# Two adjacent PSUM banks for a tile's attention values, one reciprocal and one product out of them

## The chip, the cores and the metric

The kernel runs on one core of one Trainium2 chip. A core has a matmul engine (TensorE, PE in the profile), three engines for the other arithmetic (VectorE is DVE, ScalarE is ACT, GpSimd is POOL) and SyncE (SP), which here issues transfers. The engines run side by side, each through its own list of instructions in order, and wait for each other through semaphores. TensorE writes its results into PSUM, which has eight banks of [128, 512] float32; VectorE and ScalarE carry them out to SBUF. The metric is the device time of one execution in microseconds.

## The reference

Attention with a window of 128 positions and 4 sink positions, for 4 batches, 8 heads, 768 positions and head size 64, then a normalised two-layer network with a residual:

```python
scores = scale * np.matmul(q, k.transpose(0, 1, 3, 2))
keep = is_sink | in_window            # position < 4, or 0 <= rel < 128
scores = np.where(keep, scores, -1000000000.0)
a = np.exp(scores - np.max(scores, axis=-1, keepdims=True))
a = a / (np.sum(a, axis=-1, keepdims=True) + 1e-09)
x = np.matmul(a, v)                   # then the 8 heads side by side: 512 columns
...
xn = (x - mu) / np.sqrt(var + 1e-06) * g_ln
return x + np.maximum(xn @ w_ch1, 0.0) @ w_ch2     # 512 -> 2048 -> 512
```

## The kernel before

The 3072 rows (4 batches of 768) are 24 tiles of 128 rows; two tiles are a chunk, so there are 12 chunks, three to a batch. Everything is written out, no loop is left in the program.

**Attention.** From tile 6 on, `block(t)` (L941) issues one step of TensorE for two tiles at once: the values of tile t - 1 and the scores of tile t. The scores go into two tiles of PSUM called `pair`, two banks each (L1008, L1016); ScalarE takes their exponential (L1026) and VectorE multiplies it with the band mask (L1031). The values (L981, L988, L997) go into two one-bank tiles of PSUM from the ring `one`, four heads in each: 4 x 65 columns, of which the 65th of each head is the sum of the weights. VectorE takes the reciprocal of these sums (L1049) and multiplies the values with it (L1051), for each half of the heads on its own. Then follow the statistics (L902, L904), the power on POOL (L913), the normalised row xc (L916) and, through a transposing transfer, the input `xnt` of the network. The step is named sc or sv with the tile's number, its readers rc and x. The first tiles take other functions (`attend_tile`, `attend` and `value`, L861); for tiles 4 and 5 `value` already puts both halves into one `pair` tile and empties it with one reciprocal and one product (L892, L894).

**The network.** `mlp(c)` (L1056) computes the first product of a chunk in eight groups ph of 8 matmuls (L1067), each group in one `one` bank, each emptied by a relu rl (L1078 on ScalarE, L1080 on VectorE) into `h`. The second product is done plainly for the first three chunks (L1214, emptied at L1223 with the residual in the same instruction), and for the chunks after them in seven products P1 to P7 of half the size (`second_by_seven`, L1087; matmuls at L1118). Their operands are sums of halves of `h` (s1 to s4, L1095) and of the weights (w2t, L1258, in the buffers natf and natp). Three `one` banks hold the products; copies k1, k6, k5 and o12 (L1125) and sums o11, o22, o21 (L1129) empty them, and o (L1159) adds the residual.

**Banks.** PSUM is wholly given out: banks 0 to 3 are two `pair` tiles, banks 4 to 7 four `one` tiles, each a tile of its own (L414). Value halves, groups ph, products P, transposes and other small things share the four `one` tiles.

**The order.** Nothing of the order is fixed by hand. Every step is registered with `P.op` with its engine or engines, a priority, what it reads and writes and the buffers it holds. `Plan.run` (L116) then walks through planned time with planned durations, takes the step that is ready (or the best by priority within a short window) on the engine that comes first, and gives it a slot of each ring that it needs. `Plan.lat` (L108) says how long after its producer a step may begin in the plan; `PAR` (L236) holds the priorities and allowances. The result is one order for each engine and the choice of ScalarE or VectorE for steps that either can do. The layer below writes the instructions in that order and gives each the semaphore waits that follow from what earlier instructions did with the same tile. The plan's own times are not in the program.

Of the kernel before, what the change touches and what calls it, by code (L numbers as in the profile page):

```python
# [7 lines left out]
FP32 = mybir.dt.float32  # L8
BF16 = mybir.dt.bfloat16
AF = mybir.ActivationFunctionType  # L10
ALU = mybir.AluOpType
# [54 lines left out]
class Plan:  # L66
# [41 lines left out]
    def lat(self, src, dst):  # L108
        if src.eng == "PE" and src.dma is None:
            return -self.PE_DRAIN if dst == "PE" else self.SEM  # L110
        late = PAR["late"].get(src.name[:3], 0.0) if src.dma is not None and dst == "PE" else 0.0
        return late + (self.TO_PE if dst == "PE" else self.SEM)

    WINDOW = {"PE": 0.3, "ACT": 0.25, "DVE": 0.25, "POOL": 0.25, "SP": 0.0}

# [92 lines left out]
def dve(n, per=1.04):  # L208
    t = 0.067 + 0.001 * per * n
    return (t, t + 0.09)  # L210


def fix(occ, extra=0.09):
    return (occ, occ + extra)
# [18 lines left out]
NEVER = -1e9  # L233
BIG = 3.3e38

PAR = dict(late={"trx": 2.5, "trk": 2.5, "trq": 2.5, "w2l": 0.5}, solo={8: 4.0, 10: 4.0}, bh=12, k_nb={(5, "k", 0): 53.0, (5, "k", 1): 53.0, (5, "q", 0): 53.0, (5, "q", 1): 53.0}, vs1=33.0, s4=0.9, w2t_pool=0, cut=(1, 2), rs_nb={4: 48.0, 5: 48.0}, v_nb={8: 49.0, 9: 52.0}, last7=1, opool=0, gk=(5, 4), gv=(4, 5), strict=400.0, win=0.4, tr=-8.0, sc=-5.0, sc1=-2.0, av=2.0, blk=-8.0, step=8.0, trx=9.0, by_dma=4, x_by_dma=3,  # L236
           w1p=(1.6, 2.6, 2.7, 2.8), pm=3, w2p=(4.5, 4.51, 4.52, 4.53), apart=2, vs0=(2.0, 13.0), by_tile=0, vp=(0.0, 0.1, 2.0, 2.1, 4.55, 4.56), ld1=0.05, t0=0.8, warm=7.9, pm0=-40.0, w1g=17.0, gtt=1.25, seven=3, lead=(0, 0, 0, 2, 6, 8), w2t=-4.0, at7=(0.5, 1.5, 2.5, 3.5, 4.5, 6.5, 7.5))


def general(tc, nc, slots, pairs, ones, ident_f, ident, w1, w2, mhalf, g_s, g_r, q, k, v, out, scale):  # L240
# [133 lines left out]
def kernel(  # L374
# [12 lines left out]
    nc = tc.nc  # L387
# [18 lines left out]
    psum = ctx.enter_context(tc.tile_pool(name="psum", bufs=1, space=bass.MemoryType.PSUM))  # L406
    P = Plan()

    def ring(name, n, shape, dtype, pool=consts):
        P.ring(name, [Slot(pool.tile(shape, dtype, name=f"{name}{i}"), f"{name}{i}") for i in range(n)])  # L410

    banks = [Unit() for _ in range(8)]
    pairs = [psum.tile([128, 2, 512], FP32, name=f"pair{i}") for i in range(2)]
    ones = [psum.tile([128, 512], FP32, name=f"one{i}") for i in range(4)]  # L414
    P.ring("pair", [Slot(pairs[i], f"pair{i}", banks[2 * i:2 * i + 2]) for i in range(2)])
    P.ring("one", [Slot(ones[i], f"one{i}", [banks[4 + i]]) for i in range(4)])
    ring("natf", 2, [128, H, 2, 64], FP32)
    ring("natc", 4, [128, 2, 4, 64], BF16)
    ring("nat", 8, [128, H, 64], BF16)
# [36 lines left out]
    rec, low = const("rec", [128, NT, H], FP32), const("low", [128, NT, H], FP32)  # L456
# [16 lines left out]
    V, G = nc.vector, nc.gpsimd  # L473
# [44 lines left out]
    def negs(e):  # L518
# [9 lines left out]
        op=ALU.add, axis=mybir.AxisListType.X), ["ident"], writes=[Bc["sel"]])  # L528
# [8 lines left out]
         writes=[gr_b], dma=HW_T)  # L537
    P.op("gtt", pe(0.1), PAR["gtt"], lambda e: nc.tensor.transpose(gt_p.t[:, 0:NDM], g_rows, ident_f[0:NDM, 0:NDM]),
         reads=[gr_b, Bc["ident_f"]], writes=[gt_p])
    P.op("gtc", {"DVE": fix(0.07)}, PAR["gtt"] + 0.1, lambda e: V.tensor_copy(gt, gt_p.t[:, 0:NDM]), reads=[gt_p], writes=[Bc["gt"]])  # L540
    for h in range(H):
# [3 lines left out]
            reads=[Bc["vc"]], writes=[Bc["vcd"]], nb=3.5 + 0.55 * h)  # L545
    for b in range(B):
# [4 lines left out]
            reads=[Bc["vcd"], Bc["vc"], Bc["sel4" if b else "sel"]], writes=[Bvs[b]], nb=PAR["vs0"][1] if b == 0 else PAR["vs1"] if b == 1 else 40.0 * b)  # L551
# [14 lines left out]
    for c in range(4):  # L566
        P.op(f"w2ld{c}", {"POOL": (0.75, 0.8)}, PAR["w2p"][c], lambda e, c=c: G.dma_start(
            w2[c], moe_w_ch2[512 * c:512 * (c + 1), :].rearrange("(t p) n -> p t n", p=128)),
            writes=[Bw2[c]], dma=SW_W)
# [371 lines left out]
    def block(t, what="both"):  # L941
# [20 lines left out]
            hold += pes + ([held["ps", c]] if sinks else [])  # L962
        if last:
            lc, li, lb, lr = (t - 1) // 2, (t - 1) % 2, (t - 1) // RB, (t - 1) % RB
            po = [Buf(f"po{t - 1}{u}", "one") for u in range(2)]
            reads += last["pes"] + ([last["ps"], Bvs[lb], Bvt[lb]] if last["ps"] else [])
            reads += [vn_b[u] for u in ([t - 2, t - 1, t] if lr else [t - 1, t])]
            writes[:0] = po
            po[1].lag = 0.1
            for j, pp in enumerate(pps if fresh else ()):  # L970
                pp.lag = (0.5 if last["ps"] else 0.4) + 0.15 * j
            hold += last["made"]
# [4 lines left out]
        def go(e):  # L977
            for h in [4 * u + i for i in range(4) for u in range(2)] if last else ():
                pe_, col = at_p(h // 4, h)
                rs = slice(0, 128) if lr else slice(64 * (h // 4), 64 * (h // 4) + 64)  # L980
                nc.tensor.matmul(po[h // 4].t[:, 65 * (h % 4):65 * (h % 4) + 65], lhsT=pe_[rs, col:col + 128],  # L981
                                 rhs=vn_b[t - 1].t[rs, h, :], start=h % 4 == 0, stop=True, skip_group_check=True)
            if last and last["ps"]:
                for u in range(2):
                    for qh in range(2):
                        g = qh ^ u
                        rs = slice(64 * g, 64 * g + 64)
                        nc.tensor.matmul(po[u].t[64 * qh:64 * qh + 64, 0:260],  # L988
                                         lhsT=last["ps"].t[rs, 128 * u + 64 * li:128 * u + 64 * li + 64],
                                         rhs=(vs if g == u else vs_s)[lb][rs].rearrange("p h c -> p (h c)"),  # L990
                                         start=False, stop=True, skip_group_check=True)
            for h in [4 * u + i for i in range(4) for u in range(2)] if last else ():
                for qh in (0, 1) if lr else (1,):
                    g = qh ^ (h // 4)
                    rs = slice(64 * g, 64 * g + 64)
                    pe_, col = at_p(h // 4, h)
                    nc.tensor.matmul(po[h // 4].t[64 * qh:64 * qh + 64, 65 * (h % 4):65 * (h % 4) + 65],  # L997
                                     lhsT=pe_[rs, col + 128:col + 192], rhs=vn_b[t if qh else t - 2].t[rs, h, :],
                                     start=False, stop=True, skip_group_check=True)
            if not fresh:  # L1000
                return
            for hp in range(HP):
                u, col = hp // 2, 192 * (hp % 2)
                for g, kt, k0, c0, q0, n in ((u, kT, own, 0, own, 128), *([(1 - u, kprev, old + 64, 0, own, 128)] if r else []),
                                             *([(u, kprev, old, 128, own, 64)] if r else []), (1 - u, kT, own + 64, 128, own + 64, 64)):
                    for h2 in range(2):
                        rs = slice(64 * h2, 64 * h2 + 64)
                        nc.tensor.matmul(pps[u].t[64 * g:64 * g + 64, h2, col + c0:col + c0 + n],  # L1008
                                         lhsT=kt.t[rs, hp, k0:k0 + 64], rhs=qT.t[rs, hp, q0:q0 + n],
                                         start=col == 0 and c0 == (128 if g != u and not r else 0), stop=True, skip_group_check=True)  # L1010
            if sinks:
                for hp in range(HP):
                    for qh in range(2):
                        u = hp // 2
                        p0 = 64 * (qh ^ u) + 32 * (hp % 2)
                        nc.tensor.matmul(pps[1].t[p0:p0 + 32, u, 384 + 64 * (not r):512], lhsT=kts_b[b].t[:, hp, :],  # L1016
                                         rhs=qT.t[:, hp, :].rearrange("p (i u c) -> p u i c", i=2, u=2)[:, qh, 0 if r else 1:2],
                                         start=True, stop=True, skip_group_check=True)
# [21 lines left out]
        if last:  # L1040
            st, x, xc = last["made"]
            x_b[t - 1], xst_b[t - 1] = x, st
            rcb = Buf(f"rcb{t - 1}")
            recs.append(rcb)
            for u in range(2):
                one_rc = Buf(f"rc{t - 1}{u}")
                pv = lambda u=u: po[u].t[:, 0:260].rearrange("p (h c) -> p h c", c=65)
                rc = lambda u=u: rec[:, t - 1, 4 * u:4 * u + 4]
                P.op(f"rc{t - 1}{u}", {"DVE": fix(0.115)}, d + 0.05 + 0.002 * u, lambda e, rc=rc, pv=pv: V.reciprocal(rc(), pv()[:, :, 64]),  # L1049
                     reads=[po[u]], writes=[rcb, one_rc])  # L1050
                P.op(f"x{t - 1}{u}", {"DVE": dve(256)}, d + 0.051 + 0.002 * u, lambda e, u=u, rc=rc, pv=pv: V.tensor_tensor(  # L1051
                    x.t[:, 256 * u:256 * u + 256].rearrange("p (h c) -> p h c", c=64), pv()[:, :, 0:64],
                    rc().unsqueeze(2).to_broadcast([128, 4, 64]), op=ALU.mult), reads=[po[u], one_rc], writes=[x])
            normalise(lc, li, d - 0.06, st, x, xc)

    def mlp(c):  # L1056
# [238 lines left out]
    t = PAR["t0"]  # L1295
# [67 lines left out]
```

## Time and profile before

| | |
|---|---|
| median of 3 runs | 212.18 us (211.47 to 212.77) |
| the profiled execution | 212.08 us, of which the span from first to last instruction is 210.5 us |
| TensorE, weight loads | 202.9 us busy (96%), 169.8 us (81%) |
| VectorE, ScalarE, POOL | 163.0, 116.7, 115.3 us busy |
| granted TensorE clock | 1.000 on average |
| chain that ended last | 80% TensorE, 11% VectorE |

In the rows shown below, a row of the chain has the start and the duration in microseconds, the engine, the tile that is written, the source line and the number of instructions. A row of the groups has line, engine, operation, output <- input with partitions x elements and type, the count, then busy time in us and the mean of one in ns, then the idle time in front of them and what ended it. A row of the timeline has start, duration, engine, line and operation, and in brackets the idle time before it and its releaser. Buffer numbers are left out of names: `one` stands for each of the four.

### The profile page before, as it was taken

How to read it: one execution, taken by the hardware profiler on the slowest of the kernel's cores; microseconds unless marked ns; L12 is line 12 of the kernel's file. 1: busy time of each engine (PE TensorE's matmuls, PEld its weight loads, DVE VectorE, ACT ScalarE, POOL GpSimd, SP SyncE). 2: the span in 40 equal slices, each digit the busy share in tenths (PEclk: the TensorE clock that was granted, in tenths of full speed). 3: DMA queues.
4: the chain of work that ended last, by engine and by line, in shares of the span. 5: the costliest groups of instructions: out<-in, count | busy, mean ns of one | idle time of the engine just before them, and what ended most of it. 6: DMA issues, size and time to landing. Idle time of an engine off the chain costs nothing.

```text
span 210.5 us, 7217 instructions
## 1 busy us (share of the span) xinstructions
PE 202.9 (96%) x2971; PEld 169.8 (81%) x2971; DVE 163.0 (77%) x440; ACT 116.7 (55%) x204; POOL 115.3 (55%) x170
## 2 busy tenths in 40 slices
PE   7899999999999999999999999999999999999992
PEld 2557885678888888888888888888888888888881
DVE  5599764899889768888788788988888888863472
ACT  3788786343897175464564564573563663453610
POOL 7879842479699984855766765675542022310000
PEclk9999999999999999999999999999999999999999
DMA  5999999999999999999999999999997310310202
GB/s 152 189 185 201 190 206 203 170 168 116 153 166 148 152 186 133 98 220 129 78 182 128 103 194 117 110 200 121 129 171 67 125 29 3 128 25 0 103 25 84
DMA packets 104557, 27.82 MB, mean 132 GB/s; under 512 B 93764, under 2 KB 101576, under 8 KB 104520
## 3 DMA queue, kind: packets, MB, share of 16 engines
q0 software_dynamic: 70960, 13.18, 96.2%
q1 hardware_dynamic: 32360, 13.35, 38.1%
q10 hardware_dynamic: 1200, 0.79, 1.3%
q8 instruction: 24, 0.39, 0.8%
q14 instruction: 13, 0.11, 0.2%
HBM read 27.43 MB, written 6.29 MB: 160 GB/s over the span
## 4 chain that ended last, share of the span: by engine, by line
PE 80%; DVE 11%; DMA 3%; POOL 2%; issue 1%; ACT 1%; ACTq 0%; DVEq 0%; POOLq 0%
PE one L1067 38%; PE one L1118 23%; PE one L1214 7%; PE pair L1008 3%; DMA natf<-in_q_dram 3%; DVE st L902 2%; PE one L981 2%; PE one L988 2%; DVE x L1051 1%; DVE x L894 1%; POOL st L913 1%; PE one L997 1%; DVE ot L1223 1%; PE one L879 1%; DVE xc L909 1%
## 5 line engine op out<-in xcount | busy, mean ns | idle before, releaser
L1067 PE MATMUL one<-xnt,w 128*128 128x256 bf16 x768 | 88.8, 273 | 0.7 <-DVE ot L1223 0.5
L1067 PEld LDWEIGHTS <-w 128*128 128x128 bf16 x768 | 73.9, 98 | 10.6 <-issue 0.9
L1078 ACT ACTIVATE h<-one 128x512 bf16<-128x512 f32 x86 | 51.3, 598 | 37.9 <-PE one L1067 33.4
L666 POOL DMA_DIRECT2D vn<-in_v_dram x59 | 39.3, 687 | 10.1 <-DMA w<-in_moe_w_ch_dram 7.5
L912 POOL TENSOR_SCALAR st<-st 128x1 f32<-128x1 f32 x24 | 9.0, 376 | 48.2 <-DVE st L904 47.6
L1026 ACT ACTIVATE pe<-pair 128x768 bf16<-128x768 f32 x36 | 27.2, 809 | 13.4 <-PE pair L1008 13.1
L1118 PEld LDWEIGHTS <-h 128*128 128x128 bf16 x216 | 20.5, 98 | 3.4 <-issue 0.5
L1214 PE MATMUL one<-w,h 128*128 128x256 bf16 (+1 forms) x160 | 23.1, 294 | 0.0
L1118 PEld LDWEIGHTS <-sb 128*128 128x128 bf16 x176 | 17.1, 98 | 2.1 <-DVE sb L1095 0.2
L1214 PEld LDWEIGHTS <-h 128*128 128x128 bf16 x160 | 15.1, 98 | 4.6
L1118 PE MATMUL one<-w,h 128*128 128x256 bf16 x144 | 18.7, 273 | 0.0
L1125 ACT COPY tx<-one 128x256 f32<-128x256 f32 x17 | 6.3, 372 | 22.4 <-PE one L1118 22.4
L913 POOL TENSOR_TENSOR st<-st,mhalf 128x1 f32<-128x1 f32 x24 | 16.5, 688 | 2.0
L902 DVE BATCH_NORM_STATS2 st<-x 128x6 f32<-128x512 bf16 x24 | 16.7, 694 | 0.8
L1051 DVE TENSOR_TENSOR x<-one,rec 128x256 bf16<-128x256 f32 x36 | 15.2, 421 | 0.9
L724 POOL DMA_DIRECT2D nat<-in_k_dram x16 | 15.0, 939 | 1.3 <-DMA natp<-in_q_dram 1.3
L724 POOL DMA_DIRECT2D nat<-in_q_dram x16 | 14.2, 899 | 0.0
L1159 DVE TENSOR_TENSOR ot<-ot,x 128x512 f32<-128x512 f32 x15 | 10.4, 692 | 4.3 <-ACT ot L1125 4.0
L916 DVE TENSOR_SCALAR xc<-x,st 128x512 bf16<-128x512 bf16 x18 | 7.4, 412 | 8.0 <-POOL st L913 7.9
L1031 DVE TENSOR_TENSOR pe<-pe,band 128x768 bf16<-128x768 bf16 x24 | 12.1, 541 | 1.3 <-ACT pe L1026 1.2
L1118 PE MATMUL one<-natf,sb 128*128 128x256 bf16 x92 | 12.5, 273 | 0.0
L1118 PEld LDWEIGHTS <-natc 128*128 128x128 bf16 x112 | 10.9, 98 | 1.4 <-DVE natc L1095 0.2
(149 smaller groups left out, 305.2 us busy)
## 6 DMA issues: line engine op xcount, KB each, us to landing
out_dram<-ot SPq DMA_DIRECT2D x22, 256.0 KB
w<-in_moe_w_ch_dram POOLq DMA_DIRECT2D x6, 512.0 KB, 12.6
nat<-in_k_dram POOLq DMA_DIRECT2D x16, 128.0 KB, 4.5
nat<-in_q_dram POOLq DMA_DIRECT2D x16, 128.0 KB, 6.7
vn<-in_v_dram POOLq DMA_DIRECT2D x44, 32.0 KB, 5.3
w<-in_moe_w_ch_dram POOLq DMA_DIRECT2D x4, 256.0 KB, 11.1
vn<-in_v_dram POOLq DMA_DIRECT2D x15, 64.0 KB, 5.2
natp<-in_k_dram POOLq DMA_DIRECT2D x3, 256.0 KB, 12.3
```

The lines of the kernel that those rows point to most:

```text
L666: P.op(f"vld{t}_{i}", {"POOL": (0.8, 0.85)}, prio + 0.001 * i, lambda e, p0=p0, n=n, hs=hs, src=src: G.dma_start(m.t[p0:p0 + n, hs, 0:64], ...
L724: lambda e, nat=nat, ap=ap: G.dma_start(nat.t, ap), writes=[nat], dma=SW_N, after=gate(c), nb=PAR["k_nb"].get((c, nm, i), 0.0))
L902: P.op(f"bn{t}", {"DVE": fix(0.60)}, d + 0.12, lambda e: V.bn_stats(st.t[:, 8:14], x.t), reads=[x], writes=[st, mv])
L913: G.tensor_tensor(st.t[:, 16:17], st.t[:, 17:18], mhalf, op=ALU.pow)),
L1026: nc.scalar.activation(pes[j].t.rearrange("p a b -> p (a b)")[:, 0:768].rearrange("p (a b) -> p a b", a=2), pps[j].t[:, :, 0:384], AF.Exp, ...
L1031: V.tensor_mul(at_s, at_s, band[j] if r > 1 else edge[r][j].unsqueeze(1).to_broadcast([128, 4, 192]))
L1051: P.op(f"x{t - 1}{u}", {"DVE": dve(256)}, d + 0.051 + 0.002 * u, lambda e, u=u, rc=rc, pv=pv: V.tensor_tensor(x.t[:, 256 * u:256 * u + 256 ...
L1067: nc.tensor.matmul(ph.t[:, 256 * s:256 * s + 256], lhsT=w1[ht // 4][:, j, 128 * (ht % 4):128 * (ht % 4 + 1)], rhs=xnt.t[:, j, :], start=j ...
L1078: nc.scalar.activation(dst, ph.t, AF.Relu)
L1118: nc.tensor.matmul(bank.t[:, 0:256], lhsT=left[p](m)[:, a, :], rhs=right[p](m)[:, a, :], start=new and m + a == 0, stop=m + a == 4, skip_g ...
L1159: V if e == "DVE" else G).tensor_tensor(ot[i].t, ot[i].t, x.t, op=ALU.add), reads=[ot[i], *oo[i], x], writes=[done])
L1214: nc.tensor.matmul(pc.t[:, part], lhsT=h1[s].t[:, 256 * ii + 128 * i:256 * ii + 128 * i + 128], rhs=w2[s][:, ii, sl.start + part.start:sl. ...
```

## The change

The four one-bank tiles become slices of one tile `four` of four banks, and a third ring `two` on the same banks has its three adjacent pairs. A tile's values (from tile 6 on) take one slot of `two` instead of two slots of `one`, and leave it by one reciprocal of [128, 8] and one product of [128, 512] instead of two of each. In the plan, a step of TensorE that reads what VectorE or ScalarE made is set 0.15 or 0.1 us later (after planned time 24); one that reads a transposing transfer is set 0.5 us earlier; the priority of a chunk's second block moves by 1 and that of the weight sums by 4.

```diff
+        slack = PAR["slack"].get(src.eng, 0.0) if src.dma is None and dst == "PE" and src.start > 24.0 else 0.0
-        return late + (self.TO_PE if dst == "PE" else self.SEM)
+        return late + slack + (self.TO_PE if dst == "PE" else self.SEM)
...
-PAR = dict(late={"trx": 2.5, "trk": 2.5, "trq": 2.5, "w2l": 0.5}, ... step=8.0, ... w2t=-4.0, ...)
+PAR = dict(slack={'DVE':.15,'ACT':.1}, late={"trx": 2.0, "trk": 2.0, "trq": 2.0, "w2l": 0.5}, ... step=9.0, ... w2t=-8.0, ...)
...
-    ones = [psum.tile([128, 512], FP32, name=f"one{i}") for i in range(4)]
+    four = psum.tile([128, 4, 512], FP32, name="four")
+    ones = [four[:, i, :] for i in range(4)]
     P.ring("pair", [Slot(pairs[i], f"pair{i}", banks[2 * i:2 * i + 2]) for i in range(2)])
     P.ring("one", [Slot(ones[i], f"one{i}", [banks[4 + i]]) for i in range(4)])
+    P.ring("two", [Slot(four[:, i:i + 2, :], f"two{i}", banks[4 + i:6 + i]) for i in range(3)])
...
-            po = [Buf(f"po{t - 1}{u}", "one") for u in range(2)]
+            po = Buf(f"po{t - 1}", "two")
...
-            writes[:0] = po
-            po[1].lag = 0.1
+            writes[:0] = [po]
...
-                nc.tensor.matmul(po[h // 4].t[:, 65 * (h % 4):65 * (h % 4) + 65], lhsT=pe_[rs, col:col + 128],
+                nc.tensor.matmul(po.t[:, h // 4, 65 * (h % 4):65 * (h % 4) + 65], lhsT=pe_[rs, col:col + 128],
...
-            for u in range(2):
-                one_rc = Buf(f"rc{t - 1}{u}")
-                pv = lambda u=u: po[u].t[:, 0:260].rearrange("p (h c) -> p h c", c=65)
-                rc = lambda u=u: rec[:, t - 1, 4 * u:4 * u + 4]
-                P.op(f"rc{t - 1}{u}", {"DVE": fix(0.115)}, d + 0.05 + 0.002 * u, lambda e, rc=rc, pv=pv: V.reciprocal(rc(), pv()[:, :, 64]),
-                     reads=[po[u]], writes=[rcb, one_rc])
-                P.op(f"x{t - 1}{u}", {"DVE": dve(256)}, d + 0.051 + 0.002 * u, lambda e, u=u, rc=rc, pv=pv: V.tensor_tensor(
-                    x.t[:, 256 * u:256 * u + 256].rearrange("p (h c) -> p h c", c=64), pv()[:, :, 0:64],
-                    rc().unsqueeze(2).to_broadcast([128, 4, 64]), op=ALU.mult), reads=[po[u], one_rc], writes=[x])
+            one_rc = Buf(f"rc{t - 1}")
+            pv = lambda: po.t[:, :, 0:260].rearrange("p a (h c) -> p a h c", c=65)
+            rc = lambda: rec[:, t - 1, :].rearrange("p (a h) -> p a h", a=2)
+            P.op(f"rc{t - 1}", {"DVE": fix(0.13)}, d + 0.05, lambda e: V.reciprocal(rc(), pv()[:, :, :, 64]), reads=[po], writes=[rcb, one_rc])
+            P.op(f"x{t - 1}", {"DVE": dve(512)}, d + 0.051, lambda e: V.tensor_tensor(
+                x.t.rearrange("p (a h c) -> p a h c", a=2, c=64), pv()[:, :, :, 0:64],
+                rc().unsqueeze(3).to_broadcast([128, 2, 4, 64]), op=ALU.mult), reads=[po, one_rc], writes=[x])
```

More of the change, by code (lines that the diff above doesn't have):

```diff
@@ L234 @@
 BIG = 3.3e38
-PAR = dict(late={"trx": 2.5, "trk": 2.5, "trq": 2.5, "w2l": 0.5}, solo={8: 4.0, 10: 4.0}, bh=12, k_nb={(5, "k", 0): 53.0, (5, "k", 1): 53.0, (5, "q", 0): 53.0, (5, "q", 1): 53.0}, vs1=33.0, s4=0.9, w2t_pool=0, cut=(1, 2), rs_nb={4: 48.0, 5: 48.0}, v_nb={8: 49.0, 9: 52.0}, last7=1, opool=0, gk=(5, 4), gv=(4, 5), strict=400.0, win=0.4, tr=-8.0, sc=-5.0, sc1=-2.0, av=2.0, blk=-8.0, step=8.0, trx=9.0, by_dma=4, x_by_dma=3,
-           w1p=(1.6, 2.6, 2.7, 2.8), pm=3, w2p=(4.5, 4.51, 4.52, 4.53), apart=2, vs0=(2.0, 13.0), by_tile=0, vp=(0.0, 0.1, 2.0, 2.1, 4.55, 4.56), ld1=0.05, t0=0.8, warm=7.9, pm0=-40.0, w1g=17.0, gtt=1.25, seven=3, lead=(0, 0, 0, 2, 6, 8), w2t=-4.0, at7=(0.5, 1.5, 2.5, 3.5, 4.5, 6.5, 7.5))
+PAR = dict(slack={'DVE':.15,'ACT':.1}, late={"trx": 2.0, "trk": 2.0, "trq": 2.0, "w2l": 0.5}, solo={8:4.0,10:4.0}, bh=12, k_nb={(5, "k", 0): 53.0, (5, "k", 1): 53.0, (5, "q", 0): 53.0, (5, "q", 1): 53.0}, vs1=33.0, s4=0.9, w2t_pool=0, cut=(1, 2), rs_nb={4: 48.0, 5: 48.0}, v_nb={8: 49.0, 9: 52.0}, last7=1, opool=0, gk=(5, 4), gv=(4, 5), strict=400.0, win=0.4, tr=-8.0, sc=-5.0, sc1=-2.0, av=2.0, blk=-8.0, step=9.0, trx=9.0, by_dma=4, x_by_dma=3,
+           w1p=(1.6, 2.6, 2.7, 2.8), pm=3, w2p=(4.5, 4.51, 4.52, 4.53), apart=2, vs0=(2.0, 13.0), by_tile=0, vp=(0.0, 0.1, 2.0, 2.1, 4.55, 4.56), ld1=0.05, t0=0.8, warm=7.9, pm0=-40.0, w1g=17.0, gtt=1.25, seven=3, lead=(0,0,0,2,6,8), w2t=-8.0, at7=(0.5, 1.5, 2.5, 3.5, 4.5, 6.5, 7.5))
 def general(tc, nc, slots, pairs, ones, ident_f, ident, w1, w2, mhalf, g_s, g_r, q, k, v, out, scale):
@@ L987, in go @@
                         rs = slice(64 * g, 64 * g + 64)
-                        nc.tensor.matmul(po[u].t[64 * qh:64 * qh + 64, 0:260],
+                        nc.tensor.matmul(po.t[64 * qh:64 * qh + 64, u, 0:260],
                                          lhsT=last["ps"].t[rs, 128 * u + 64 * li:128 * u + 64 * li + 64],
@@ L996, in go @@
                     pe_, col = at_p(h // 4, h)
-                    nc.tensor.matmul(po[h // 4].t[64 * qh:64 * qh + 64, 65 * (h % 4):65 * (h % 4) + 65],
+                    nc.tensor.matmul(po.t[64 * qh:64 * qh + 64, h // 4, 65 * (h % 4):65 * (h % 4) + 65],
                                      lhsT=pe_[rs, col + 128:col + 192], rhs=vn_b[t if qh else t - 2].t[rs, h, :],
```

## The prediction

> **What bounds the kernel now.** I read the page's table of engines first, then the chain of work that ended last, then the timeline of one chunk.
>
> ```profile
> span 210.5 us, 7217 instructions
> PE 202.9 (96%) x2971; PEld 169.8 (81%) x2971; DVE 163.0 (77%) x440; ACT 116.7 (55%) x204; POOL 115.3 (55%) x170
> ```
>
> ```profile
> 17.60 0.43 PE one L1067 x3
> ...
> 56.86 0.67 DVE ot L1223
> 57.57 3.65 PE one L1067 x32
> ...
> 88.51 6.22 PE one L1067 x56
> ...
> 104.09 6.22 PE one L1067 x56
> ...
> 119.02 0.35 PE pair L1008 x32
> 119.37 0.23 PE pair L1016 x8
> 119.59 6.22 PE one L1067 x56
> ...
> 134.87 6.22 PE one L1067 x56
> ...
> 150.46 6.22 PE one L1067 x56
> ...
> 165.96 6.22 PE one L1067 x56
> ...
> 180.88 6.22 PE one L1067 x56
> ...
> 206.35 0.43 DVE ot L1168
> ```
>
> The columns are start, duration, engine, tile and line. From 88.51 to 180.88 the chain is TensorE and little else: six chunks in 92.37 us, some 15.4 each. TensorE is the bound, and every other engine works beside it. What lets it run on is that four one-bank tiles rotate:
>
> ```profile
> 104.03 6.29 PE L1067 MATMUL one<-xnt,w 128*128 128x256 bf16 x56
> ...
> 105.11 0.69 DVE L1080 TENSOR_SCALAR h<-one 128x512 bf16<-128x512 f32 x1 [0.37 <-PE one L1067]
> ...
> 105.99 0.60 ACT L1078 ACTIVATE h<-one 128x512 bf16<-128x512 f32 x1 [0.41 <-PE one L1067]
> ```
>
> TensorE writes 56 matmuls, seven groups of 8, without a pause, one step each (6.29 - 0.27) / 55 = 0.109 us (0.27 is one matmul's own length, below). A group is 0.87 us. VectorE and ScalarE empty finished groups meanwhile, each in a bank that TensorE is not filling. The first reader starts at 105.11; group one ended by the model at 104.03 + 7 x 0.109 + 0.27 = 105.06. So a hand-off from TensorE costs 0.04 us behind the drain of a last matmul, which is 0.27 - 0.11 = 0.16. The way back is in the chain above: 56.86 + 0.67 = 57.53, and TensorE starts at 57.57, again 0.04. A full turn costs 0.16 + 0.04 + 0.04 = 0.24 us beside the reader.
>
> **The change part by part.** The merged reciprocal and product are the small part. Readers' prices, by the groups of instructions (busy, mean ns):
>
> ```profile
> L1067 PE MATMUL one<-xnt,w 128*128 128x256 bf16 x768 | 88.8, 273 | 0.7 <-DVE ot L1223 0.5 <-issue 0.2
> L1078 ACT ACTIVATE h<-one 128x512 bf16<-128x512 f32 x86 | 51.3, 598 | 37.9 <-PE one L1067 33.4 <-DVE sb L1095 1.3 <-DVE st L902 1.1
> L1051 DVE TENSOR_TENSOR x<-one,rec 128x256 bf16<-128x256 f32 x36 | 15.2, 421 | 0.9
> L1129 DVE TENSOR_TENSOR ot<-one,tx 128x256 f32<-128x256 f32 x24 | 9.4, 417 | 2.4 <-PE one L1118 1.6 <-ACT tx L1125 0.9
> L1080 DVE TENSOR_SCALAR h<-one 128x512 bf16<-128x512 f32 x10 | 6.9, 690 | 3.1 <-ACT qT L671 1.5 <-PE one L1067 1.5
> L1125 ACT COPY tx<-one 128x256 f32<-128x256 f32 x17 | 6.3, 372 | 22.4 <-PE one L1118 22.4
> L1049 DVE RECIPROCAL rec<-one 128x4 f32<-128x4 f32 x36 | 6.2, 173 | 0.5 <-PE one L997 0.4
> L1223 DVE SCALAR_TENSOR_TENSOR ot<-one,st,x 128x512 f32<-128x512 f32 x6 | 4.5, 744 | 0.6 <-PE one L1214 0.5
> L894 DVE TENSOR_TENSOR x<-pair,rec 128x512 bf16<-128x512 f32 x2 | 1.4, 691 | 0.1
> L892 DVE RECIPROCAL rec<-pair 128x8 f32<-128x8 f32 x2 | 0.4, 194 | 0.0
> ```
>
> Before, a tile costs 2 x (0.173 + 0.421) = 1.19 us of VectorE; the merged form is already there for two tiles, 0.194 + 0.691 = 0.89. Over 18 tiles that is 18 x 0.30 = 5.4 us of an engine that is not the bound. The plan's parameters move every odd block (scores of tile 13, say) behind P1, the last operand sum s4 in front of reciprocal and product, the weight sums (w2t) some steps forward, and seven copies k1 from VectorE to ScalarE; TensorE's 2971 matmuls stay the same. What this could win is TensorE's own stalls: 134.87 to 150.46 (15.59) has the work of 119.59 to 134.87 (15.28) and takes 0.31 longer, 88.51 to 104.09 (15.58) has one such place more, and the products at 57.57 begin 0.48 late. Together some 1.1 us. On the queues of SP and POOL six transfers and one pair of small POOL operations change places with a neighbour, each with chunks of lead: nothing.
>
> **The large part is the tile itself.** The four banks are now one tile of [128, 4, 512], of which the old names are slices. The waits that the built programs carry, resolved to the operation that gives the awaited count (P, ph: products; rl, k, o, x: readers; the bank in brackets):
>
> ```
> before                               changed
> ph4_3 [3] waits x of tile 11 [3]     ph4_3 [0] waits rl4_1 [2]
> rl4_2 [1] waits ph4_2 [1]            rl4_2 [3] waits ph4_3 [0]
> ph4_4 [0] waits rl4_1 [0]            ph4_4 [1] waits rl4_2 [3]
> rl4_3 [3] waits ph4_3 [3]            rl4_3 [0] waits ph4_4 [1]
> ph4_5 [2] waits x of tile 11 [2]     ph4_5 [2] waits rl4_3 [0]
> ```
>
> Before, each wait is for its own bank. In the changed program 190 waits of TensorE and 195 of readers are for another bank; before it is none. Whatever touched the tile last, on another engine, is awaited, so the four banks behave as one: product, drain, reader, next product. Behind a waiting matmul stand all later ones in TensorE's order, and for them the readers.
>
> I count this walk in the changed program's order from stage to stage. Added time = readers now in series + 0.24 per turn - TensorE's work on the other PSUM tiles, which a reader still covers (0.35 and 0.23, rows L1008 and L1016 above).
>
> Six steady chunks: 42 relu on ScalarE x 0.598 = 25.1, 6 on VectorE x 0.690 = 4.1, 24 copies x 0.372 = 8.9, 18 sums x 0.417 = 7.5, 12 reciprocals with products x (0.21 + 0.69) = 10.8; together 56.4. Turns: 98 x 0.24 = 23.5. Covered: 4.7; stalls of before that dissolve, 0.6. Added **74.6**, or 15.4 -> 27.8 per chunk.
>
> From 17.60 to 88.51: 28 relu on ScalarE 16.7, 5 on VectorE 3.5, 6 wide sums x 0.744 = 4.5, 5 merged and 3 old reciprocals with products 6.3, 4 copies and 3 sums 2.7, two transposes emptied on ScalarE and two on VectorE 4.4, one exponential 0.4; 38.5. Turns 50 x 0.24 = 12.0. Covered 5.0, stalls gone 1.5. Added **44.0**.
>
> From 180.88 to the end: 15 relu 9.0, 4 copies 1.5, 12 sums 5.0, one reciprocal with product 0.9; 16.4. Turns 29 x 0.24 = 7.0, less 0.6 that stands there already at the end. Added **22.8**.
>
> Up to 17.60 the same walk has 15 turns and 10.9 us of readers, of which the late inputs and the score products cover most. Estimate **6**, between 3 and 9.
>
> Sum: 6 + 44.0 + 74.6 + 22.8 = 147.4. The profiled execution took 212.08 us (span 210.5), the median shown is 212.18. Forecast 212.08 + 147.4 = 359.5, so **360 us**.
>
> What is uncertain: the turn, between 0.16 (drain wholly hidden by the model) and 0.35, over 192 turns -15 to +21; the start, 3 either way; readers held back in VectorE's queue by the product xc, which waits for POOL:
>
> ```profile
> DVE xc L916 <- POOL st L913: 7.9, 16, 0.9
> ```
>
> This is at nothing in my sum, because more than 4 us of the slower walk lie between a tile's product x and the next reader behind xc; with the cover gone it is some 8 us. The range 335 to 395 holds these bounds.
>
> [...]
>
> **The rivals.** (1) Not slower: the waits for other banks do not bind. Then only the stalls go: 212.08 - 1.1 = 211.0 us. It decides at one place: if products of a chunk stay 0.87 apart beside readers of 0.60, this is it. For it speaks that two engines use two banks at once now; against it that a wait in the program is a wait on the chip. Chance 0.04.
>
> (2) TensorE also falls to its lower rate, because it pauses after each group. The trace has two rates:
>
> ```profile
> 3.53 1.91 PE L772 MATMUL pair<-neg,ident 128*128 128x512 bf16 x4
> ...
> 14.40 0.60 PE L772 MATMUL pair<-neg,ident 128*128 128x512 bf16 x2
> ...
> 16.05 0.40 PE L924 MATMUL one<-ident,xc 128*128 128x128 bf16 x4 [0.40 <-DVE xc L909]
> ```
>
> Four matmuls in 1.91 against two in 0.60 is about 0.43 each against 0.22, although the page shows a full clock in both. TensorE's work on the walk is some 174 us; at half rate for half of it, 360 + 87 = 447. Against it: pauses of 0.40 at 16.05 and of 0.48 at 57 changed nothing, and the new ones are 0.7 to 1.3. [...] Chance 0.08.
>
> (3) Part of the walk is shorter than counted, say a third of the readers lie beside work that I put in series: 111 us of readers / 3 = 37, so 323. Against it: the waits name every neighbour. Chance 0.06.
>
> **How the numbers follow.** Forecast 0.82, rivals 0.04, 0.08, 0.06. The range 335 to 395 keeps 0.82. Within 1%, about what a measurement of this kernel can tell from no change, lies only rival one: same 0.04. Slower 0.95, faster 0.01 for what of rival one comes out better.
>
> **What would show it.** PE's busy share falls from 96% to some 60%; the relu's idle time in front becomes larger than its work and TensorE's idle time names relu, copies and sums as releasers; groups of L1067 stand 1.7 us apart instead of 0.87 (0.87 + 0.60 + 0.24); the chain alternates PE with ACT and DVE. VectorE's busy time falls by some 5 us. Wrong would be a chunk near 15.4 us (rival one), matmul steps of 0.21 in the chunks (rival two), or pauses of TensorE shorter than its reader.

## The result, and the profile after

The changed kernel takes **376.42 us** in the median (371.86 to 378.61), the kernel before 212.02 us on the same chip (211.47 to 212.77): a ratio of **1.768, 95% interval 1.751 to 1.785**. Forecast were 360 us, between 335 and 395. The profiled execution took 378.61 us, its span is 377.1; it was the slowest of the four, with the lowest mean clock, 0.914.

The head of the page of the changed kernel: span, busy time of the engines, TensorE's busy tenths and its granted clock in 40 slices of 9.4 us.

```profile
span 377.1 us, 7173 instructions
...
PE 248.3 (66%) x2969; PEld 181.8 (48%) x2971; DVE 162.0 (43%) x397; ACT 119.3 (32%) x211; POOL 115.8 (31%) x170
...
PE   6857667887687666666766666666756656656664
...
PEclk9585558999659999999899999999899999999999
```

TensorE was busy for 96% and is now for 66%. For most of the first sixth of the span, and once more near 100 us, its clock was at half (the windows from 30 to 60 and from 100 to 110 us show 0.50), which the page of before does not show anywhere (1.000 on average). The chain that ended last, in chunk 6 (start, duration, what):

```profile
187.15 1.05 PE four L1067 x8
188.20 0.02 issue
188.22 0.60 ACT h L1078
188.83 0.04 issue
188.87 1.05 PE four L1067 x8
189.94 0.60 ACT h L1078
190.54 0.04 issue
190.59 1.05 PE four L1067 x8
```

Where before 56 matmuls ran in one piece of 6.22 us, there is one group of eight, its reader, the next group. From 187.15 to 188.87 it is 1.72 us. The groups of instructions, with the idle time in front of them, and the list of waits (total, times, longest) say who waits for whom:

```profile
L1067 PE MATMUL four<-xnt,w 128*128 128x256 bf16 x768 | 110.5, 294 | 57.5 <-ACT h L1078 30.9
L1078 ACT ACTIVATE h<-four 128x512 bf16<-128x512 f32 x85 | 50.4, 597 | 145.2 <-PE four L1067 102.6
L1051 DVE TENSOR_TENSOR x<-four,rec 128x512 bf16<-128x512 f32 x18 | 12.5, 692 | 3.9 <-PE four L1118 3.4
L1050 DVE RECIPROCAL rec<-four 128x8 f32<-128x8 f32 x18 | 3.7, 208 | 20.2 <-PE four L1214 6.3 <-PE four L1067 5.8 <-ACT pe L1028 5.4
```

```profile
ACT h L1078 <- PE four L1067: 102.6, 57, 6.1
PE four L1067 <- ACT h L1078: 30.9, 45, 1.3
PE four L1118 <- ACT h L1078: 17.8, 26, 0.7
```

TensorE waits for the relu 45 times in front of a product, and the relu for TensorE 57 times; before, TensorE sat idle 0.7 us in front of all L1067 together. The products (L1118) wait for the relu 26 times; the list of the kernel before has no such wait.

The stages end at the same operations as in the prediction. Rows of the chain that open them, in the changed kernel:

```profile
27.94 1.88 PE four L1067 x8
54.72 1.88 PE four L1067 x8
125.20 1.92 PE four L1067 x16
154.37 1.05 PE four L1067 x8
325.26 1.05 PE four L1067 x8
```

| stage | before | after | added | added, second profile | forecast |
|---|---|---|---|---|---|
| up to the first product of the feed-forward part | 17.6 | 27.9 | 10.3 | 11.4 | 6 |
| from there to the second product of chunk 4 | 70.9 | 126.4 | 55.5 | 47.3 | 44.0 |
| six steady chunks | 92.4 | 170.9 | 78.5 | 77.4 | 74.6 |
| to the end of the span | 29.6 | 51.9 | 22.3 | 22.3 | 22.8 |

The second profile is a later one of the same kernel, 370.39 us long with a mean clock of 0.944; its rows 29.03, 147.26 and 317.03 stand with the experiments on the clock below.

The sum is 166.6 in the first profile and 158.4 in the second, forecast 147.4. The steady chunks and the end, with a granted clock of 0.98 and 1.00 in the first profile (windows from 154 to 326 and from 326 to 377 us), come within 4 us; the two early stages, with a clock of 0.50 for 58.0 us of the first profile, carry 15.8 of the 19.2 that are missing in the first profile and 8.7 of the 11.0 in the second.

### The profile page after: what moved, and what is told of

The parts are those of the page before. It is cut to its first block, busy times and chain, and to the rows that moved or that the text cites. A ratio compares the mean times of both kernels' runs of the same rounds, so it can differ in the third digit from the quotient of the medians.

```text
span 377.1 us, 7173 instructions
## 1 busy us (share of the span) xinstructions
PE 248.3 (66%) x2969; PEld 181.8 (48%) x2971; DVE 162.0 (43%) x397; ACT 119.3 (32%) x211; POOL 115.8 (31%) x170
## 4 chain that ended last, share of the span: by engine, by line
PE 63%; ACT 18%; DVE 14%; issue 4%; ACTq 0%; DVEq 0%
PE four L1067 29%; PE four L1118 18%; ACT h L1078 14%; PE four L1214 6%; DVE x L1051 3%; ACT tx L1125 2%; DVE ot L1129 2%; DVE h L1080 2%; PE four L983 1%; DVE ot L1223 1%; DVE rec L1050 1%; PE four L990 1%; ACT pe L1028 1%; PE pair L775 1%; PE four L882 1%
## 5 line engine op out<-in xcount | busy, mean ns | idle before, releaser
L1067 PE MATMUL four<-xnt,w 128*128 128x256 bf16 x768 | 110.5, 294 | 57.5 <-ACT h L1078 30.9
L1067 PEld LDWEIGHTS <-w 128*128 128x128 bf16 x768 | 79.6, 104 | 85.2 <-issue 70.9
L1078 ACT ACTIVATE h<-four 128x512 bf16<-128x512 f32 x85 | 50.4, 597 | 145.2 <-PE four L1067 102.6
L1118 PEld LDWEIGHTS <-h 128*128 128x128 bf16 x216 | 21.3, 99 | 30.3 <-issue 27.8
L1118 PE MATMUL four<-w,h 128*128 128x256 bf16 x144 | 21.5, 271 | 17.2 <-ACT h L1078 12.3
L1214 PE MATMUL four<-w,h 128*128 128x256 bf16 (+1 forms) x158 | 23.4, 293 | 6.2 <-DVE h L1080 2.8
L1118 PEld LDWEIGHTS <-sb 128*128 128x128 bf16 x176 | 17.0, 97 | 20.9 <-issue 18.4
L1125 ACT COPY tx<-four 128x256 f32<-128x256 f32 x24 | 8.9, 372 | 54.1 <-PE four L1118 20.4
L1129 DVE TENSOR_TENSOR ot<-four,tx 128x256 f32<-128x256 f32 x24 | 10.2, 425 | 27.8 <-ACT tx L1125 10.1
L1214 PEld LDWEIGHTS <-h 128*128 128x128 bf16 x160 | 15.2, 98 | 11.3 <-issue 6.8
L1118 PEld LDWEIGHTS <-natc 128*128 128x128 bf16 x112 | 10.8, 97 | 14.2 <-issue 12.6
L1080 DVE TENSOR_SCALAR h<-four 128x512 bf16<-128x512 f32 x11 | 7.6, 692 | 23.2 <-ACT h L1078 10.4
L1118 PE MATMUL four<-natf,sb 128*128 128x256 bf16 x88 | 12.2, 272 | 4.3 <-DVE x L1051 3.7
L1118 PE MATMUL four<-natp,h 128*128 128x256 bf16 x72 | 12.1, 295 | 4.2 <-ACT ot L1125 3.7
```

What stands on the lines that cost most here:

```text
L1067: nc.tensor.matmul(ph.t[:, 256 * s:256 * s + 256], lhsT=w1[ht // 4][:, j, 128 * (ht % 4):128 * (ht % 4 + 1)], rhs=xnt.t[:, j, :], start=j ...
L1078: nc.scalar.activation(dst, ph.t, AF.Relu)
L1080: V.tensor_scalar_max(dst, ph.t, 0.0)
L1118: nc.tensor.matmul(bank.t[:, 0:256], lhsT=left[p](m)[:, a, :], rhs=right[p](m)[:, a, :], start=new and m + a == 0, stop=m + a == 4, skip_g ...
L1125: return P.op(f"{name}_{c}", {"ACT": act(256), "DVE": dve(256)}, d, lambda e: (nc.scalar.copy if e == "ACT" else V.tensor_copy)(dst(), ban ...
L1129: return P.op(f"{name}_{c}", {"DVE": dve(256, 1.06)}, d, lambda e: V.tensor_tensor(dst(), bank.t[:, 0:256], kept.t, op=ALU.add), reads=[ba ...
```

## The experiments

Theory: one tile for four banks makes every access wait for the last one on another engine, and these waits are the loss. Rivals: the merged pair and its adjacent banks; the new due times and order; TensorE's clock.

**One part alone.** First the kernel before with nothing but the tile:

```
-    ones = [psum.tile([128, 512], FP32, name=f"one{i}") for i in range(4)]
+    four = psum.tile([128, 4, 512], FP32, name="four")
+    ones = [four[:, i, :] for i in range(4)]
```

> The kernel before with nothing changed but its four one-bank tiles, which become slices of one four-bank tile: no merged reciprocal or product, old parameters, old order. In the built program 201 waits of TensorE on readers and 193 waits of readers on TensorE are then for another bank (0 or a few before). If the shared tile is the whole cause: 350 to 390 us, with groups of eight matmuls 1.7 us apart. If the merged pair (its need of two adjacent banks) is the cause: 212 us. If the new plan is the cause: 212 us.

It took 389.12 us, ratio 1.841 (1.830 to 1.851). The tile alone costs more than the whole change. Then the plan alone:

```
-        return late + (self.TO_PE if dst == "PE" else self.SEM)
+        slack = PAR["slack"].get(src.eng, 0.0) if src.dma is None and dst == "PE" and src.start > 24.0 else 0.0
+        return late + slack + (self.TO_PE if dst == "PE" else self.SEM)
...
-PAR = dict(late={"trx": 2.5, ...
+PAR = dict(slack={'DVE':.15,'ACT':.1}, late={"trx": 2.0, ...
```

> The kernel before with the change's parameters and its later due times alone; four tiles and two reciprocals and two products as before. If the shared tile is the whole cause: 210 to 213 us, a ratio of 0.99 to 1.005. If the new plan is what costs: more than 250 us.

210.25 us against 211.26, ratio 0.9959 (0.9936 to 0.9982): the plan costs nothing, it gains 1.0 us. This is the fastest kernel of the study.

**The waits alone.** The changed kernel's instructions and order stay; after they are written out, the edges between accesses to different banks on different engines are taken away, except where the two also share other data:

```
+        for (e, b), (g, members) in groups.items():
+            if e != i.engine and not b & banks:
+                keep = [j for j, r, w in members if not (write.isdisjoint(r) and write.isdisjoint(w) and read.isdisjoint(w))]
+                tc.declare_no_dep(i, group=g, keep=keep, reason="other banks")
```

Here b and banks are the banks that the earlier and the present instruction touch.

> The changed kernel, instruction for instruction and in its own order, but each wait between accesses to different banks of the shared tile is taken out (same-bank waits stay, and so does every wait for data in another tile): 193 waits of TensorE, 185 of readers on TensorE, 61 of readers on readers go. If these waits are the whole cause: 209 to 213 us, the steady chunk back at 15.4 us, and the granted clock at 1.00 after the start. If the merge, its adjacent banks or the new plan cost by themselves: 230 us or more. If TensorE's lower clock was there for another reason than the pauses: 225 to 230 us.

211.61 us, ratio 1.0018 (0.9999 to 1.0038). All of the 165 us are in these waits. The page of this run:

```profile
span 210.0 us, 7158 instructions
...
PE 201.6 (96%) x2969; PEld 169.7 (81%) x2971; DVE 157.4 (75%) x397; ACT 119.4 (57%) x211; POOL 115.4 (55%) x170
...
PEclk9999999999999999999999999999999999999999
```

and of its chain the rows of two steady chunks:

```profile
104.13 6.22 PE four L1067 x56
...
119.58 6.22 PE four L1067 x56
```

The same instructions again stand 56 in a row, and a chunk is 119.58 - 104.13 = 15.45 us. With the pauses the half clock is gone too: its mean is 1.000 in the profiled execution, and 9 tenths or more in every slice.

**One half of the waits.** The condition above was narrowed to TensorE's own waits, then to the readers' (`i.engine == PE`, `i.engine != PE`).

> The changed kernel in its own order, with TensorE's 193 waits on readers of other banks taken out; the readers' 185 waits on TensorE's work in other banks and 61 waits on each other stay. If the loss is a closed ring (a reader waits for the product issued before it, the next product for that reader), opening it on one side must give nearly all back, since TensorE then runs ahead by the four banks: 211 to 235 us. If each kind of wait costs by itself in proportion to its number: 290 to 310 us.

> The changed kernel in its own order, with the readers' waits on other banks taken out (185 on TensorE, 61 on each other); TensorE's waits on readers of other banks stay (196). If the loss is a closed ring: 212 to 260 us, since a reader now runs beside the next product and is done before the product after that, which waits for it; what is left are stalls behind readers that queue on their engine. If TensorE's waits are the loss by themselves: 340 us or more.

229.77 us, ratio 1.089 (1.087 to 1.092), and 235.66 us, ratio 1.120 (1.114 to 1.127). Either half, taken out alone, gives back some 147 or 141 of the 165 us. So it isn't the number of waits but the ring: a reader waits for the product that was issued before it, into whatever bank, and the next product waits for that reader. With TensorE's side open, the timeline of TensorE shows the run of 56 again, a little stretched:

```profile
129.59 6.60 PE L1067 MATMUL four<-xnt,w 128*128 128x256 bf16 x56
```

Then the tile was cut in two tiles of two banks:

```
-    four = psum.tile([128, 4, 512], FP32, name="four")
-    ones = [four[:, i, :] for i in range(4)]
+    halves = [psum.tile([128, 2, 512], FP32, name=f"half{i}") for i in range(2)]
+    ones = [halves[i // 2][:, i % 2, :] for i in range(4)]
...
+    P.ring("two", [Slot(halves[i], f"two{i}", banks[4 + 2 * i:6 + 2 * i]) for i in range(2)])
```

> The changed kernel with the shared tile cut in two tiles of two banks, so that the pair ring has two places instead of three; the planner sets its order anew. Waits for another bank: 100 of TensorE, 67 of readers on TensorE, 35 of readers on each other, all inside a half. If the loss is a closed ring over all accesses of one tile: products that alternate between the halves leave the ring open, 215 to 290 us. If what costs is that a tile has more than one bank at all: 340 us or more.

234.70 us, ratio 1.113 (1.110 to 1.116). Two tiles of two banks are not free, but the ring is open for most of the time: products that go to the other half need not wait for the reader. The order is not that of the changed kernel here, since the plan was made anew. The run of 56 stands in this timeline too:

```profile
131.81 6.29 PE L1067 MATMUL half<-xnt,w 128*128 128x256 bf16 x56
```

**What the merge itself costs.** With the old plan, and the waits between banks taken out as above:

> The merged reciprocal and product in the shared tile, waits between different banks taken out, with the old parameters and due times: what the merge alone is worth. If the merge saves what the rows of before give (5.4 us of VectorE, which does not bound the kernel): 211 to 213 us. If the need of two adjacent banks delays products: 214 to 220 us.

> As the merge with the old plan and without waits between different banks, but each tile's two banks are left by two reciprocals and two products again; what stays is that a tile takes two adjacent banks at once. That run took 1.0076 of the kernel before, and its TensorE waits 1.0 us and 0.7 us at the start for banks that are emptied late. If the need of adjacent banks is the price: 1.005 to 1.010 and the same two waits. If the longer merged instructions are: 0.998 to 1.003.

The merge: 212.72 us, ratio 1.0076 (1.0048 to 1.0104), inside the expected 211 to 213, yet above the kernel before. With two reciprocals and two products on the adjacent banks: 213.37 us, ratio 1.0108 (1.0083 to 1.0132), a little above the 1.005 to 1.010 expected if the adjacent banks are the price, and outside the 0.998 to 1.003 expected if the longer instructions are. So the need of two adjacent banks, with the order that the plan makes for it, costs about 2.2 us. The new plan gives 1.1 back (211.61 against 212.72). That the merged instructions give back the 0.7 between the two ratios is not shown, since the intervals overlap. TensorE's waits in the last run, and those in the kernel before for the same transposes and products:

```profile
PE four L926 <- DVE xnt L937: 1.0, 1, 1.0
PE four L1068 <- ACT xnt L938: 0.7, 1, 0.7
PE four L1068 <- DMA xnt<-xc: 0.4, 1, 0.4
```

```profile
PE one L924 <- DVE xc L909: 0.6, 2, 0.4
PE one L1067 <- DVE ot L1223: 0.5, 1, 0.5
PE one L1067 <- issue: 0.2, 1, 0.2
```

The first two waits, 1.7 us, are new and stand in both runs with adjacent banks, at the start of the kernel. The run above with the new plan and without the waits has them as well, 1.0 us in front of a transpose (L927) and 0.7 in front of a product (L1067), and takes 211.61 us. So they fit the price of 2.2 us, but that they are its cause is not shown.

**The clock.** Does TensorE's half clock come from the pauses, and is it the missing 19 us? Matmuls on constants were put ahead of each first write of a bank, into that bank, so that they fill the pause. Their own waits for other banks, and those of others for them, are left out as above; all other waits of the changed kernel stay:

```
+                if o.eng == "PE" and 4.0 < o.start < 1000000000.0:
+                    for b in new:
+                        flat = b.t if b.ring == "one" else b.t[:, 0, :]
+                        for _ in range(5):
+                            fillers.add(nc.tensor.matmul(flat[:, 0:256], lhsT=junk[:, 0:128], rhs=junk[:, 0:256], start=True, stop=True).ins.name)
```

> The changed kernel with all its waits, and five matmuls of 256 columns on constants issued ahead of each first write of a bank, into that bank, which waits for nothing but the bank's own last reader; the product behind them overwrites their values. They take up some 0.5 us of the 0.7 us pause at the full rate. If the 15 to 19 us that the sum missed are TensorE's halved clock and the pauses bring it on: a granted clock of 0.98 or more, groups of eight matmuls at 1.05 us everywhere, 355 to 370 us in all. If the clock is halved for another reason: clock 0.90 to 0.94, and 385 to 400 us, since the added matmuls then take longer than the pause. If the halved clock costs nothing: 376 us or a little more.

396.07 us, ratio 1.878 (1.871 to 1.884), with the clock at 0.994: neither expectation as a whole. With the pauses filled the half clock is all but gone (0.994 to 1.000 in four executions), as it is in the run without the pauses (1.000), against 0.914 in the first profile of the changed kernel. So in this kernel it goes with the pauses; but five added matmuls don't fit in every pause. They make up 12% of the chain that ended last, some 47 us of its span of 395.2. So four of them, ahead of 57 first writes in the early part alone, beside the changed kernel once more:

> As the run with added matmuls, but four of them instead of five and only ahead of the 57 first writes that the plan puts between 4 and 62 us (to about the start of chunk 3), so that they stay inside the pause and end where the changed kernel's clock is full again by itself. If the halved clock of that stretch is worth the 15 to 19 us that the sum missed: first products of chunk 3 at 92 to 97 us instead of 109.8, 355 to 366 us in all. If it is worth less, the start of chunk 3 tells how much. If the clock is halved as soon as the added matmuls end: chunk 3 later by the same amount, 370 to 378 us in all.

> The changed kernel once more, beside the run with early added matmuls: 372 to 379 us, and a halved clock between 10 and 60 us as in its first profile, if that is a property of the kernel; a clock near 1.00 there if it was an accident of one execution.

370.77 us (369.35 to 371.08) and 373.33 us (370.39 to 380.0). The changed kernel came as expected, with the half clock again in the early part (0.53 from 10 to 50 us, in the rows below). With early added matmuls the time lies in the range that was set for a clock that halves as soon as they end, but the clock is 1.00 in every window up to 110 us and 0.991 over the whole profile. The expected 355 to 366 did not come, and chunk 3 began at 117.35, not before 97: that number, and the 109.8 beside it, rested on a wrong count of matmuls; the row of the first profile that it must be held against is 125.20. The rows that open chunk 0, chunk 1 and chunk 3, first for the changed kernel's second profile (with the rows that open and end its six steady chunks), then with early added matmuls:

```profile
29.03 1.88 PE four L1067 x8
...
53.58 1.05 PE four L1067 x8
...
118.08 1.92 PE four L1067 x16
...
147.26 1.05 PE four L1067 x8
...
317.03 1.05 PE four L1067 x8
```

```profile
29.10 1.05 PE four L1067 x8
...
48.24 1.05 PE four L1067 x8
...
117.35 1.92 PE four L1067 x16
```

Between 10 and 50 us the windows of the two profiles show busy time, and the granted clock as the third figure from the end:

```profile
10.00:50.00 40.00, 27.61 (x264) 17.60 (x261) 13.13 (x34) 14.60 (x24) 15.72 (x23) 0.53 1.05 134
```

```profile
10.00:50.00 40.00, 34.16 (x413) 25.42 (x413) 17.65 (x60) 15.69 (x26) 20.13 (x29) 1.00 1.24 151
```

Chunk 0 takes 24.55 us where the clock is at half for most of it (0.50 from 30 to 40 us, 0.62 from 40 to 50), and 19.14 with added matmuls and a full clock (1.00): the clock is worth 5.4 us there at least, if the added matmuls only cost time. Chunks 1 and 2 have a clock of 1.00 in both, in every window from 50 to 110 us, and take 64.50 and 69.11: the added matmuls cost 4.6 us of their own and eat the gain. In the first profile chunks 1 and 2 took 125.20 - 54.72 = 70.48, 6.0 more than in the second, with the clock at half up to 60 us, in the start of chunk 1 (0.50), and from 97 to 111 us (0.52).

The time of the changed kernel goes with this clock: the four executions beside the added matmuls took 370.39 and 370.47 us with a mean clock of 0.944, 376.18 with 0.927 and 380.0 with 0.905. That is 9.6 us for 0.039; carried on to a full clock, an estimate, some 357 us. One of the four executions before them doesn't fit (376.83 with 0.982). The chain of the first profile gives a second estimate:

```profile
33.09 1.88 PE four L1067 x8
...
35.64 0.59 PE four L927 x4
```

At half the clock a group, its reader and the two hand-offs take 35.64 - 33.09 = 2.55 us where they take 1.72 at the full one, so 0.83 of 2.55 is lost. The clock is at half for 64.8 us of the first profile and 41.0 of the second; that makes 21 and 13 us, and leaves 357 us from either. With added matmuls, which cost time themselves, it is 370.8. So by these estimates the changed kernel at a full clock lies between 357 and 370.8, and the forecast of 359.5 does too; no run says closer.

## Why the prediction was right, and where it was off

- **The tile as the large part**: shown. Without the waits for other banks the time is 211.61; rival one had 211.0 for waits that don't bind. The later count of the waits for another bank, 193 of TensorE, 185 of readers on TensorE and 61 of readers on each other, differs from the 190 and 195 of the prediction, but the sum does not use it.
- **The turn of 0.24 us and a group every 1.7 us**: 1.72 measured, made of 1.05 (0.87 and the drain), 0.60 and about 0.07. The walk's terms for the chunks (74.6) and the end (22.8) came out at 78.5 and 22.3.
- **The start, "Estimate 6, between 3 and 9"**: 10.3, and 11.4 and 11.5 in the two later profiles, the last with a full clock (1.00 up to 30 us) and added matmuls. Less was covered there than assumed: this term was too small by some 5 us, the largest single miss in the second profile. Why isn't shown; the run with a full clock there speaks against the clock, but its added matmuls cost time of their own.
- **44.0 for the second stage**: 55.5. Here the sum left the clock at full and put the half rate into a rival as all or nothing (447 us, chance 0.08). It came in part. By the rows above it was at least 5.4 in chunk 0, 2.2 more where chunk 0 took 26.78 instead of 24.55, and 6.0 in chunks 1 and 2: 13.6 us, more than the 11.5 that are missing. In the second profile the stage added 47.3, 3.3 more than forecast, and the clock was worth at least 5.4 of that. So the step that failed here is the term for the clock, which was nothing; the walk itself was, if anything, 2 us too long in both.
- **VectorE's busy time down by some 5 us**: the page says 1.0, and yet the term is right. Product and reciprocal fell from 15.2 + 6.2 to 12.5 + 3.7, by 5.2. The page counts time in which any instruction runs. Before, the 440 durations in the trace add up to 179.7 us for 163.0 busy, so neighbours overlap; in the changed kernel 397 durations add up to 171.2 for 162.0, since they stand apart. In the run without the waits it is 157.4, 5.6 less than before.
- **The small edits**: the plan was to win up to 1.1 us and wins 1.0. The merge was costed at nothing off the bound; the two adjacent banks that it needs cost 2.2 us, which no step priced. Under the ring, where every reader is in series, the whole change took 376.4 against 389.1 with the tile alone. How much of that is the merge isn't shown, since that pair also differs in the plan's moves and in the mean clock (0.907 in the profile of the tile alone).
- **The wait of xc for POOL** stayed small: 14 waits of at most 0.5 us.

With each bank guarded by the waits for that bank alone, the changed kernel takes 211.61 us, and all of the loss is back. With the other waits it has pauses of 0.7 us between groups and a granted clock that changes between 0.50 and 1.00.

## What to carry to other kernels

A slice of a tile is guarded like the whole tile here. Before you join buffers that rotate, look in the built program which operation each wait is for; if a reader waits for the product behind its own, and the product after that waits for this reader, the rotation is gone and the time is the sum of both: here 1.72 us a group, of 1.05 and 0.60 and the hand-offs. Opening the ring at one side gave most of it back (147 or 141 of 165 us), and the pair that must be adjacent had a price of its own (2.2 us).

## What the runs showed of the hardware

TensorE's clock stayed at half for 34.1 us in one piece, although none of the pauses in the window below was longer than 1.45 us. Windows of the changed kernel's first profile (busy us of each engine, granted clock, share of the DMA engines):

```profile
30.00:60.00 30.00, 20.44 (x162) 13.20 (x161) 9.17 (x40) 6.74 (x14) 15.27 (x21) 0.50 0.94 93
195.00:225.00 30.00, 18.60 (x253) 14.15 (x252) 13.46 (x30) 9.80 (x18) 9.96 (x14) 1.00 0.65 74
```

In the first window TensorE pauses for 0.5 to 1.45 us between groups, in the second for 0.2 to 1.0. It is busy for 20.4 and 18.6 of 30 us, and its clock is 0.50 in the first and 1.00 in the second, so the share of busy time in windows of this length does not tell the clock. In the trace's own record of the clock the stretches at half last 10.2, 34.1, 13.7, 3.4 and 3.4 us in this profile and 37.5 and 3.4 in the second. (The record of the kernel before begins only at 6.6 us. The full clock that the prediction read at 3.53 us, beside matmuls of 0.43 us, is therefore not measured.)

In the ring a group and its pause are busy for 1.05 of 1.72 us at the full clock, 61%, and for 1.88 of 2.55 at half, 74%. Without the pauses the mean clock of an execution was 0.996 to 1.000, with five added matmuls in them 0.994 to 1.000, with four in the early ones 0.991 to 1.000; in the eight executions of the changed kernel it was 0.905 to 0.982. So the half clock goes with the pauses in these runs. Which pauses bring it on, and why one stretch of them stays at half and another does not, is not shown.
